# A planned order that prefers older inputs, more low parts on VectorE, and all turns of late units by DMA, in a block-sparse attention and FFN kernel

## The chip, the cores and the metric

The kernel runs on one core of a Trainium2 chip. The metric is device time of one execution in microseconds. The time of the kernel before is the median of three runs; one more execution was profiled.

## What is computed

Attention over a block mask, and an ELU feed-forward layer on its output:

```python
# q, k, v: (4, 8, 768, 64) float32 = B, H, S, D; sampled_blocks: (24, 3) int64; block = 32
scores = (1/sqrt(D)) * q @ k^T                    # per batch and head
mask   = |block_i - block_j| <= 1, or i or j the first or last block,
         or j one of the 3 blocks sampled for block row i
attn   = softmax(where(mask, scores, -1e9));  y = attn @ v
x      = y.transpose(0, 2, 1, 3).reshape(3072, 512)
h      = x @ w_in                                 # 512 x 2048, float64
g      = where(h > 0, h, exp(min(h, 0)) - 1)
out    = g @ w_out                                # 2048 x 512, float64; out (3072, 512) float32
```

## The kernel before, in words

**Split numbers.** Products are made of fp16 parts. A float is cast to fp16 (the high part) and the rest, value minus high part, is a second fp16 (the low part); a product takes three matmuls, high by high, high by low, low by high. So nearly every operand goes through two operations: a cast (`scaled`, L295 to L301, on ScalarE at L297 or on VectorE at L299) and a low part (for `p` L822, for `g` L902, for `xn` L866, for weights L462), which may run on VectorE or GpSimd. The weights are float64, decoded from their bits by ScalarE and VectorE (L427 to L463).

**Attention.** `attention` (L658) handles a unit of 128 query rows and all 8 heads. There are 24 units. Most hold two blocks of each of two batches; units 0 and 1 are of one batch; units 8 and 20 hold the first and last blocks, which attend to every key, so they have three chunks of scores (`NC = 3`, L762). Units 0 to 11 belong to the first two batches, 12 to 23 to the others. For each pair of heads (`hp`, four of them) a unit makes scores (L788, 32 narrow matmuls of 32 columns of weights, or more), their maximum (L799, VectorE), two exponentials (L817, ScalarE), the cast of `p` (L297 or L299), its low part (L822), the turn of `p` into `pT`, P·V (L837) and a sum into `x32` (L846, VectorE). At the end of a unit the rows are divided by their sums (L854 to L856), split into `xn` and turned into `xT`.

**Turns.** `turn16` (L374) turns eight 128x128 tiles of fp16. Either by the transfer engine, one DMA issued on SP (L377), or by eight TensorE transposes into a PSUM bank (L385) and an eviction by ScalarE or VectorE (L387 to L391). `via` (L951) says which: for units 0 to 3 everything on TensorE; from unit 4 on q and `xn` by DMA, and `p` of the first two head pairs (`hp < via[1]`, `PP = 2`, L825) on TensorE, of the other two by DMA.

**FFN.** `ffn` (L872) handles two units, a stage `U` of 256 rows, in eight steps: layer 1 (L885, 24 wide matmuls into `h`), ELU (L895, L897 on ScalarE, L893 on VectorE), the cast and low part of `g`, and layer 2 (L908, 6 matmuls into each of two `o` banks). At the end of a stage two evictions go into `ro` (L918) and are stored from SP (L642). There is one `ro` buffer (`rooms`, L260), so the second eviction needs the first store to have landed.

**What sets the order.** No engine's order is written out. Each operation is added with a priority (a time in us at which it is wanted, worked out from `t`, the stage's time, by constants such as `AHEAD`, `T`, `F2`, `LAG`, `K1`), with the engines it may run on and a duration on each. `Plan.order` (L70) then goes through a planned time `t` and gives each engine, when it is free, the first operation in the order of priority that is ready: its inputs ended `LATENCY` ago, and its buffers have room. An engine that isn't free in time keeps what it would finish sooner than another by a margin (L113 to L120); `MO` is the margin of low parts, and a low part goes to the engine that ends it first, with VectorE set back by it. So a change of a constant moves operations on all engines, and between them. Every engine then executes its list in order on the chip, waiting where an input isn't there.

Of the kernel before, what the change touches and what calls it, by code (L numbers as in the profile page):

```python
# [17 lines left out]

LATENCY = 0.15
LANDING = 2.5  # L20
IN_FLIGHT = 8
BACKLOG = 3.5
FETCH, FETCH_TIME = 256, 5.0
PACE, SLACK = 0.0, 0.1
SWITCH, HERD, HOLD = 0.1, 1, 0.7


# [15 lines left out]
class Plan:  # L43
# [26 lines left out]
    def order(self):  # L70
# [5 lines left out]
        made = {tag: [] for tag in self.rooms}  # L76
# [30 lines left out]
        def ready(op, eng):  # L107
# [31 lines left out]
        while left:  # L139
            moved = False  # L140
            for eng, ops in waiting.items():
# [84 lines left out]
def kernel(  # L226
# [37 lines left out]
    plan = Plan(rooms)  # L264
# [37 lines left out]

    ALONE, SPECIAL, SECOND = 1, 8, -110.0
    MO, MC, ML, MH = -0.6, 0.0, 0.5, 0.6

# [352 lines left out]
    def attention(u, t, via):  # L658
        g, i0, blocks = unit(u)
        sp = i0 == 0  # L660
        PITCH, TURN, TIMES = (PI, TU, TM) if u >= EVEN else (1.0, 2.0, 4.0)
        keys_in = [k for x in {b for b, _ in blocks} for k in kT_buf[x]]
        tq = t - 9 - AHEAD

# [22 lines left out]
        if sp:  # L687
            vts = [Buf("VT", lambda: None) for _ in range(3)]

            def take(e):  # L690
                for vt in vts:
                    vt.slot = next_slot()
                    in_room["v", vt.slot] = None
            plan.add({"SP": 0.01}, t - 8, take, new=vts, name=f"vt{u}")
            for c in range(NKC):
                vt = vts[c // 2]

                def load(e, c=c, vt=vt):
                    r0 = BLK + c * P
                    for d, xs in vd[g]:  # L700
# [6 lines left out]
                plan.add({"SP": 0.45 * len(vd[g])}, t - 8, load, r=[d for d, _ in vd[g]], w=[vt], dma=1.6, name=f"vt{u}")  # L707
            vin = vts
        else:
# [3 lines left out]
            for y in range(2):  # L713
# [7 lines left out]
                def load(e, vt=vt, parts=parts):  # L721
# [3 lines left out]
                    for d, xs, i in parts:  # L725
# [4 lines left out]
                        nc.sync.dma_start(room[BLK:P, 1], d.ap[(i - 1) * BLK : (i + 2) * BLK, :])  # L730
                plan.add({"SP": 0.6 * len(parts)}, t - 8, load, r=[d for d, _ in there], new=[vt], dma=1.8, name=f"vt{u}")
# [6 lines left out]
                plan.add({"POOL": 1.0 * len(parts)}, t - 8, gather, r=[d for d, _ in there], w=[vt], dma=1.7, land=5.0, port=False, name=f"vg{u}")  # L738

                def copy(e, kg=kg, y=y):  # L740
# [4 lines left out]
                    for x in range(2):  # L745
# [13 lines left out]
                plan.add({"POOL": 1.75 if two else 2.5}, t - 6, copy, r=keys_in, new=[kg], name=f"kg{u}")  # L759

# [162 lines left out]
    SHIFT = {"ACT": 0.6, "DVE": 0.7}  # L923
    EVEN, NEXT = 6, 14.0
    PI, TU, TM = 2.0, 3.0, 4.0
    TWO, AHEAD, T, F0, LEAD, NPE = 6, 16.0, 58.0, 60.0, 130.0, 4
    WI, WID, F2, LAG = -100.0, 3.0, 4.5, 14.0
    V1, K1 = 70.0, 16.0
    QP, PP, XP = 0, 2, 0
    zero_rows(-480)  # L930
# [10 lines left out]
    for U in range(NU // 2):  # L941
        t = F0 + T * U
        for u in (2 * U, 2 * U + 1):
            at = t - LEAD + (T / 2 if U else NEXT) * (u % 2)
            if u == NUP:
# [39 lines left out]
```

## Time and profile before

| | |
|---|---|
| median of three runs | 823.76 us (820.37 to 824.18) |
| the profiled execution: its span | 807.9 us |
| busy shares of the span: TensorE, VectorE, ScalarE, GpSimd | 88%, 63%, 53%, 49% |
| instructions | 26664 |
| moved by DMA | 120.07 MB, mean 149 GB/s |

The profile gives the profiled execution's own time as its span, from the first to the last instruction; the runs' times are some 16 us longer, as they hold what lies around the span. "Busy" is the time in which an engine executed something; the share is a mean over stages with different limits. In the page of the profile a first stretch to about 140 us, in which weights and keys are prepared, has TensorE busy for four to eight tenths; then it is busy for nine tenths and more of nearly every slice until the last one.

### The profile page before, as it was taken

What the parts mean: (1) busy time and instruction counts of PE and PEld (TensorE: products, weight loads), DVE (VectorE), ACT (ScalarE), POOL (GpSimd) and SP (SyncE); (2) the same over time, 40 slices, a digit from 0 to 9 for tenths busy, and PEclk for the clock granted to TensorE, in tenths of its full rate; (3) what the DMA queues carried; (4) which work ended last, traced back from release to release, by engine and by line L of the source; (5) the groups of instructions that cost most, each with busy time, mean ns of one, the idle gap of its engine ahead of it and who ended that gap; (6) DMA issues with size and microseconds to landing.
All of it is one profiled execution on the core that took longest, in us unless ns stands there. A gap on an engine that the chain in (4) does not pass through costs nothing.

```text
span 807.9 us, 26664 instructions
## 1 busy us (share of the span) xinstructions
PE 711.3 (88%) x11256; PEld 488.3 (60%) x11256; DVE 506.4 (63%) x854; ACT 428.9 (53%) x747; POOL 392.7 (49%) x600
## 2 busy tenths in 40 slices
PE   6445665999998999899899998999999999999993
PEld 3333553767657657567567656656667576566761
DVE  7689788998876747666478766647555566522210
ACT  4598777888545636355466525445345346322220
POOL 2587657687534347543565535445324464422120
PEclk8555578999999999999999999999999999999997
DMA  8898999988787789999459987464761698210000
GB/s 231 248 281 277 264 263 212 217 204 163 134 179 223 169 148 209 172 170 200 94 106 182 162 176 93 110 131 42 172 114 15 94 208 146 41 40 1 28 1 26
DMA packets 191064, 120.07 MB, mean 149 GB/s; under 512 B 148000, under 2 KB 168608, under 8 KB 190944
## 3 DMA queue, kind: packets, MB, share of 16 engines
q1 hardware_dynamic: 185664, 100.79, 61.0%
q0 software_dynamic: 5280, 17.58, 8.5%
q8 instruction: 88, 1.44, 0.8%
q14 instruction: 32, 0.26, 0.1%
HBM read 82.05 MB, written 13.21 MB: 118 GB/s over the span
## 4 chain that ended last, share of the span: by engine, by line
PE 66%; DMA 14%; DVE 6%; issue 4%; ACT 3%; POOL 2%; SPq 2%; POOLq 1%; DVEq 0%; ACTq 0%
PE o L908 27%; PE h L885 25%; PE s L788 5%; DMA out_dram<-ro 5%; PE w L837 3%; DMA pT<-p 2%; PE av L837 2%; DMA wo<-in_moe_w_out_dram 2%; DMA st<-in_k_dram 2%; PE av L385 2%; DMA VT<-vd 1%; PE s L385 1%; DMA st<-in_v_dram 1%; ACT e L817 1%; DVE w L451 1%
## 5 line engine op out<-in xcount | busy, mean ns | idle before, releaser
L885 PE MATMUL h<-xT,wi 128*128 128x256 f16 x2304 | 280.4, 275 | 7.8 <-DVE fe L893 4.7
L908 PE MATMUL o<-wo,g 128*128 128x512 f16 x1152 | 274.6, 381 | 0.0
L885 PEld LDWEIGHTS <-wi 128*128 128x128 f16 x2304 | 220.2, 98 | 53.9 <-issue 9.0
L902 POOL TENSOR_TENSOR g<-fe,g 128x512 f16<-128x512 f32 x79 | 96.0, 1215 | 188.8 <-DVE g L299 167.8
L908 PEld LDWEIGHTS <-g 128*128 128x128 f16 x1152 | 107.5, 98 | 109.2 <-issue 1.6
L822 POOL TENSOR_TENSOR p<-e,p 128x512 f16<-128x512 f32 x86 | 102.3, 1193 | 88.6 <-DVE p L299 44.9
L895 ACT ACTIVATE fe<-h 128x512 f32<-128x512 f32 x96 | 57.3, 597 | 148.4 <-PE h L885 145.7
L893 DVE SCALAR_TENSOR_TENSOR fe<-h,fe 128x512 f32<-128x512 f32 x96 | 66.0, 688 | 107.8 <-ACT fe L897 100.1
L817 ACT ACTIVATE e<-s,m 128x256 f32<-128x256 f32 x208 | 86.1, 471 | 68.4 <-POOL p L822 25.4
L757 POOL COPY kG<-kT 128x128 int32 x264 | 76.3, 331 | 41.6 <-PE s L788 18.6
L799 DVE TENSOR_REDUCE m<-s 128x2 f32<-128x512 f32 x104 | 69.8, 685 | 36.0 <-PE s L788 35.7
L735 POOL DMA_INDIRECT VT<-vd,idx x66 | 65.5, 992 | 27.6 <-issue 9.1
L837 PEld LDWEIGHTS <-pT 128*32 128x32 f16 x3456 | 42.8, 97 | 47.3 <-issue 34.6
L897 ACT ACTIVATE fe<-fe,gs 128x512 f32<-128x512 f32 x96 | 69.3, 722 | 2.4
L788 PE MATMUL s<-kG,qT 128*32 128x160 f16 x704 | 44.5, 249 | 10.6 <-ACT e L817 6.3
L788 PEld LDWEIGHTS <-qT 128*32 128x32 f16 x1664 | 33.2, 101 | 28.9 <-issue 21.5
L846 DVE TENSOR_REDUCE x<-w 128x130 f32<-128x260 f32 x64 | 27.2, 425 | 33.6 <-PE w L837 33.2
L788 PE MATMUL s<-kT,qS 128*32 128x96 f16 (+1 forms) x832 | 48.2, 226 | 0.0
L788 PE MATMUL s<-kT,qT 128*32 128x96 f16 (+1 forms) x832 | 48.1, 227 | 0.0
L788 PE MATMUL s<-kG,qS 128*32 128x160 f16 x704 | 44.2, 248 | 4.0 <-DVE qS L299 2.7
L299 DVE CAST p<-e 128x512 f16<-128x512 f32 x54 | 32.4, 603 | 19.2 <-ACT e L817 6.3
L385 PEld LDWEIGHTS <-p 128*128 128x128 f16 x512 | 34.5, 105 | 15.9 <-POOL p L822 7.7
(134 smaller groups left out, 859.9 us busy)
## 6 DMA issues: line engine op xcount, KB each, us to landing
VT<-vd SPq DMA_DIRECT2D x44, 195.0 KB
VT<-vd SPq DMA_DIRECT2D x22, 390.0 KB
wo<-in_moe_w_out_dram SPq DMA_DIRECT2D x12, 512.0 KB
out_dram<-ro SPq DMA_DIRECT2D x21, 256.0 KB
st<-in_q_dram SPq DMA_DIRECT2D x40, 128.0 KB
wo<-in_moe_w_in_dram SPq DMA_DIRECT2D x9, 512.0 KB
st<-in_moe_w_in_dram SPq DMA_DIRECT2D x7, 512.0 KB
VT<-vd SPq DMA_DIRECT2D x12, 260.0 KB
```

Source lines behind the costliest of these rows:

```text
L735: nc.gpsimd.indirect_dma_start(VT[0:96, 2 * vt.slot, xs[0] : xs[-1] + 1].rearrange("p b x -> p (b x)"), None, d.ap, bass.IndirectOffsetOnA ...
L757: nc.gpsimd.tensor_copy(dst[:, :, r * 16 : (r + 1) * 16], src[:, :, bass.ds(at[r], 16)])
L788: nc.tensor.matmul(dst, lhsT=qq.ap[:, h, j * BLK : (j + 1) * BLK], rhs=mv, start=first, stop=(y == 1 and qq is qS and o0 + w == 256))
L799: nc.vector.tensor_reduce(m.ap[:, 2 * c : 2 * c + 2] if sp else m.ap[:, 6:8], ss[c].ap, axis=AX.X, op=ALU.max, negate=True)
L817: nc.scalar.activation(e32.ap[:, y, :], ss[c].ap[:, y, :], AF.Exp, bias=m.ap[:, 6 + y : 7 + y])
L822: plan.add(LO, t + PITCH * hp + 1, margin=MO, fn=lambda e, e32=e32, p=p: ENG[e].tensor_tensor(p.ap[:, 1, :], flat(e32.ap), p.ap[:, 0, :], ...
L837: nc.tensor.matmul(av.ap[j * BLK : (j + 1) * BLK, y, v0:], lhsT=pts[c].ap[:, pl * 4 + y * 2 + z, j * BLK : (j + 1) * BLK], rhs=VT[:, room, ...
L885: nc.tensor.matmul(h.ap[:, a, :], lhsT=w[:, wl, cs], rhs=x.ap[:, xl, cc, :], start=(n == 0), stop=(n == 3 * NCC - 1))
L893: nc.vector.scalar_tensor_tensor(e32.ap, h.ap, -IH * GS, e32.ap, op0=ALU.mult, op1=ALU.min)
L897: plan.add({"ACT": 0.68}, p0 + 2.6, lambda e, e32=e32: nc.scalar.activation(e32.ap, e32.ap, AF.Relu, bias=gs_col, scale=-GS), r=[e32], w=[ ...
L902: plan.add(LO, p0 + 2.6, margin=MO, fn=lambda e, e32=e32, g=g: ENG[e].tensor_tensor(g.ap[:, 1], e32.ap, g.ap[:, 0], op=ALU.subtract), r=[e ...
L908: nc.tensor.matmul(o.ap, lhsT=g.ap[:, gl, f % 2, m * P : (m + 1) * P], rhs=wo[f][:, wl, :], start=(f == 0 and n == 0), stop=(f == NFC - 1 ...
```

## The change

The constants go to the top of the file, and most change a little. Four things are new:

- `eased`: in the planned time behind `EASE_FROM = 140`, an operation of TensorE whose inputs from other engines ended less than 1.04 us ago (3.03 for a DMA), or whose buffer came free so recently, gets 10 added to its rank. So one whose inputs were ready for longer goes first, if there is one.
- `TURNED = 14`: from unit 14 on no head pair's `p` is turned on TensorE. Units 4 to 13 stay as they were.
- `MARGIN`: `MO`, the margin of low parts, goes from -0.6 to -0.06. The other three stay.
- The assumed latency between engines goes from 0.15 to 0.04, the backlog of transfers from 3.5 to 1.72, and the stages are ranked by new constants (`AHEAD`, `T`, `F2`, `LAG`, `WID`, `K1`, and the time of q).

```diff
-LATENCY = 0.15
+LATENCY = 0.04
-BACKLOG = 3.5
+BACKLOG = 1.72
+MARGIN = (-0.06, 0.0, 0.5, 0.6)
+PITCH1 = (2.0, 3.16, 4.0)
+TWO, AHEAD, T, F0, LEAD, NPE = 6, 17.58, 60.83, 60.0, 130.0, 4
+WI, WID, F2, LAG = -100.0, 2.93, 4.73, 15.05
+TURNED = 14
+EASE, EASE_DMA, EASE_FROM = 1.04, 3.03, 140.0
...
+        def eased(op):
+            for d in op.deps:
+                if d.eng != "PE" and d.end + (EASE_DMA if d.dma else EASE) > t:
+                    return False
+            for b in op.new:
+                if b.tag is None:
+                    continue
+                i = len(made[b.tag]) - self.rooms[b.tag]
+                if i >= 0 and any(o.end + EASE > t for o in (*made[b.tag][i].writers, *made[b.tag][i].readers) if o.eng != "PE"):
+                    return False
+            return True
...
                         s = fetch(op)[0] + hurry(op) + (0.0 if op.narrow or not narrow or HERD < 2 else SWITCH)
+                        if t > EASE_FROM and not eased(op):
+                            s += 10.0
...
-    MO, MC, ML, MH = -0.6, 0.0, 0.5, 0.6
+    MO, MC, ML, MH = MARGIN
...
-        tq = t - 9 - AHEAD
+        tq = t - QLEAD - AHEAD
...
-    TWO, AHEAD, T, F0, LEAD, NPE = 6, 16.0, 58.0, 60.0, 130.0, 4
-    WI, WID, F2, LAG = -100.0, 3.0, 4.5, 14.0
...
-            attention(u, at, ("PE", 4, "PE") if u < NPE else (("DMA", "PE")[QP], PP, ("DMA", "PE")[XP]))
+            attention(u, at, ("PE", 4, "PE") if u < NPE else ("DMA", 2 if u < TURNED else 0, "DMA"))
```

Lines behind the constants stand 26 lower in the changed file: L385 becomes L411, L822 L848, L902 L928, L885 L911.

How this moves instructions, at three places. First the SP queue around units 16 and 17 (`pT` is the turned `p`, `VT` gathered values, `st` loaded rows of q, `out_dram` the result). Before:

```order
L377 DMA_TRANSPOSE pT_11203<-p_11089 128x8x128
L377 DMA_TRANSPOSE pT_11280<-p_11166 128x8x128
L642 DMA out_dram<-ro_11241 2x64x512
L642 DMA st_11404<-in_q_dram 64x8x64 x2
L730 DMA VT<-vd_191 96x2080 x2
L377 DMA_TRANSPOSE pT_11643<-p_11592 128x8x128
L377 DMA_TRANSPOSE qT_11698<-n_10626 128x8x128
L377 DMA_TRANSPOSE pT_11798<-p_11739 128x8x128
```

And after the change:

```order
L403 DMA_TRANSPOSE pT_11060<-p_11029 128x8x128
L403 DMA_TRANSPOSE pT_11118<-p_11058 128x8x128
L403 DMA_TRANSPOSE qT_11170<-n_10084 128x8x128
L668 DMA out_dram<-ro_11135 2x64x512
L403 DMA_TRANSPOSE xT_10719<-xn_11225 128x8x128
L403 DMA_TRANSPOSE pT_11327<-p_11235 128x8x128
L403 DMA_TRANSPOSE pT_11357<-p_11249 128x8x128
L756 DMA VT<-vd_192 96x2080 x2
L403 DMA_TRANSPOSE pT_11648<-p_11525 128x8x128
L403 DMA_TRANSPOSE pT_11692<-p_11584 128x8x128
```

Unit 17 has four turns of `p` in the queue instead of two, and the output store stands behind two turns of `p` and one of q.

Second, VectorE in unit 17, at the operations for `p` and for `g` of the stage beside it. Before:

```order
L893 SCALAR_TENSOR_TENSOR fe_11337<-h_11282,fe_11337 128x512
L299 CAST g_11352<-fe_11337 128x512
L497 SCALAR_TENSOR_TENSOR n_11317<-st_9858,n_11317 128x8x64
L846 TENSOR_REDUCE x_11149<-w_11356 128x130
L822 TENSOR_TENSOR p_11354<-e_11299,p_11354 128x512
L299 CAST p_11417<-e_11348 128x512
L893 SCALAR_TENSOR_TENSOR fe_11415<-h_11322,fe_11415 128x512
```

And after the change:

```order
L919 SCALAR_TENSOR_TENSOR fe_11392<-h_11208,fe_11392 128x512
L325 CAST g_11436<-fe_11392 128x512
L928 TENSOR_TENSOR g_11436<-fe_11392,g_11436 128x512
L825 TENSOR_REDUCE m_11487<-s_11403 128x2
L825 TENSOR_REDUCE m_11523<-s_11440 128x2
L848 TENSOR_TENSOR p_11525<-e_11331,p_11525 128x512
L325 CAST p_11584<-e_11352 128x512
L848 TENSOR_TENSOR p_11584<-e_11352,p_11584 128x512
```

Before, the low parts of `g_11352` and `p_11417` were on GpSimd; now each follows its cast on VectorE. In the whole program 143 low parts go that way: of `p` 86 are on GpSimd before and 20 now, of `g` 79 and 27, of `xn` 11 and 2, of weights 19 and 3. TensorE has 192 transposes fewer.

Third, ScalarE at the two evictions at the end of stage 7 (`ro` is the buffer of which there is one, `fe` and `g` belong to ELU steps of the next stage, `n` to a cast of q, `e` to exponentials). Before:

```order
L895 ACTIVATE fe_13370<-h_13283 128x512
L897 ACTIVATE fe_13370<-fe_13370,gs 128x512
L297 ACTIVATE g_13421<-fe_13370 128x512
L297 ACTIVATE ro_13425<-o_12634 128x512
L895 ACTIVATE fe_13441<-h_13357 128x512
L817 ACTIVATE e_13444<-s_13305,m_13355 128x256 x2
```

And after the change:

```order
L921 ACTIVATE fe_12920<-h_12828 128x512
L923 ACTIVATE fe_12920<-fe_12920,gs 128x512
L323 ACTIVATE n_12932<-st_12841 128x8x64
L323 ACTIVATE ro_13041<-o_12260 128x512
L323 ACTIVATE n_13094<-st_12909 128x8x64
L323 ACTIVATE ro_13112<-o_12290 128x512
L921 ACTIVATE fe_13147<-h_13080 128x512
L923 ACTIVATE fe_13147<-fe_13147,gs 128x512
```

Before, one of the two evictions was on ScalarE and the other on VectorE; now both are on ScalarE, one cast apart.

## Rows read from the trace of the kernel before

**Rows 1.** Busy time of each engine by window. The columns: the window, its length, busy time of PE, PEld, DVE, ACT and POOL with the number of instructions, the granted TensorE clock, the busy share of the DMA engines, GB/s.

```profile
60.00:193.00 133.00, 99.49 (x1976) 72.91 (x1976) 118.17 (x176) 107.50 (x188) 93.17 (x146) 0.80 0.96 234
...
0.00:100.00 100.00, 53.28 (x897) 39.92 (x897) 80.81 (x132) 71.22 (x117) 61.08 (x130) 0.59 0.91 260
100.00:140.00 40.00, 25.45 (x565) 19.20 (x565) 34.69 (x52) 30.72 (x54) 26.83 (x38) 0.80 1.05 241
140.00:193.00 53.00, 52.13 (x929) 36.60 (x927) 47.69 (x76) 44.71 (x82) 37.60 (x64) 0.99 0.92 202
193.00:720.00 527.00, 505.86 (x8377) 344.37 (x8375) 327.12 (x568) 263.30 (x468) 250.41 (x358) 1.00 0.73 137
720.00:808.00 88.00, 74.58 (x496) 48.23 (x493) 16.14 (x29) 18.93 (x29) 16.81 (x15) 0.95 0.05 16
```

**Rows 2.** The page: busy time and share of each engine, then the chain of waits by engine.

```profile
PE 711.3 (88%) x11256; PEld 488.3 (60%) x11256; DVE 506.4 (63%) x854; ACT 428.9 (53%) x747; POOL 392.7 (49%) x600
...
PE 66%; DMA 14%; DVE 6%; issue 4%; ACT 3%; POOL 2%; SPq 2%; POOLq 1%; DVEq 0%; ACTq 0%
```

**Rows 3.** TensorE's waits from 150 to 808 us, the first five of fourteen rows: the operation that waited, what it waited for, us in total, times, longest.

```profile
PE s L385 <- DVE n L497: 3.6, 2, 3.0
PE h L885 <- DVE g L299: 3.0, 1, 3.0
PE av L837 <- DVE pT L299: 2.7, 2, 2.1
PE w L837 <- DMA pT<-p: 2.5, 2, 1.4
PE s L788 <- DVE fe L893: 1.6, 1, 1.6
```

**Rows 4.** The chain of waits, pieces of the stretches around 245 us and around 480 us (start, length, what).

```profile
245.57 10.40 DMA out_dram<-ro
...
480.09 10.91 DMA out_dram<-ro
491.02 0.60 ACT ro L297
491.62 0.62 ACT fe L897
492.26 0.70 DVE fe L893
492.98 0.44 DVE g L299
493.74 4.09 PE h L885 x36
```

**Rows 5.** The chain of waits, single pieces between 427 and 455 us.

```profile
427.96 0.45 PE s L788 x26
...
435.73 1.29 PE o L908 x6
437.02 0.46 PE w L837 x32
437.48 1.42 PE h L885 x12
438.90 0.45 PE av L385 x8
...
441.69 0.55 PE av L385 x8
442.25 0.56 PE s L788 x32
...
454.68 1.31 PE h L885 x12
```

**Rows 6.** Groups of instructions by line and shape, whole span: count, busy us, mean ns of one, idle time before them and what ended it.

```profile
L385 PE MATMUL av<-ident,p 128*128 128x128 f16 x256 | 19.7, 220 | 0.2 <-PE w L837 0.2
L297 ACT ACTIVATE pT<-av 128x1024 f16<-128x1024 f16 x27 | 27.6, 1023 | 12.0 <-PE av L385 11.5 <-issue 0.4
L822 DVE TENSOR_TENSOR p<-e,p 128x512 f16<-128x512 f32 x26 | 23.2, 891 | 2.7 <-issue 1.5 <-ACT p L297 1.0
L299 DVE CAST p<-e 128x512 f16<-128x512 f32 x54 | 32.4, 603 | 19.2 <-ACT e L817 6.3 <-DMA pT<-p 5.0 <-PE s L385 3.1
L799 DVE TENSOR_REDUCE m<-s 128x2 f32<-128x512 f32 x104 | 69.8, 685 | 36.0 <-PE s L788 35.7
L817 ACT ACTIVATE e<-s,m 128x256 f32<-128x256 f32 x208 | 86.1, 471 | 68.4 <-POOL p L822 25.4 <-DVE m L799 24.6 <-PE o L908 7.0
```

**Rows 7.** The tiles `p`, `g` and `pT`: count, duration in ns (min, median, max), first and last start.

```profile
L822 POOL TENSOR_TENSOR p<-e,p x86: 1142/1160/1650, 43.8 to 693.3; 128x512 f16<-128x512 f32 x86
L299 DVE CAST p<-e x54: 413/427/2577, 44.5 to 688.6; 128x512 f16<-128x512 f32 x54
L377 SPq DMA_TRANSPOSE pT<-p x48: 1231/1316/5028, 157.7 to 694.4; - x48
L822 DVE TENSOR_TENSOR p<-e,p x26: 674/692/1741, 96.5 to 681.8; 128x512 f16<-128x512 f32 x26
...
L902 POOL TENSOR_TENSOR g<-fe,g x79: 1145/1156/1672, 135.6 to 788.4; 128x512 f16<-128x512 f32 x79
L902 DVE TENSOR_TENSOR g<-fe,g x17: 680/693/1531, 144.3 to 566.8; 128x512 f16<-128x512 f32 x17
```

**Rows 8.** Turns by DMA: two pieces of the chain of waits, then SP's timeline of unit 20 (start, length in the queue, count).

```profile
545.36 9.02 DMA pT<-p
...
678.40 10.13 DMA pT<-p
...
623.82 3.39 SPq L377 DMA_TRANSPOSE pT<-p  x2
627.33 1.26 SPq L377 DMA_TRANSPOSE qT<-n  x1
630.93 11.37 SPq L377 DMA_TRANSPOSE pT<-p  x4
```

**Rows 9.** The chain of waits where stage 1 begins.

```profile
183.18 1.01 PE s L788 x64
184.18 2.73 PE h L885 x24
```

More of the change, by code (lines that the diff above doesn't have):

```diff
@@ L17 @@
 WINDOW = 1
-LATENCY = 0.15
+LATENCY = 0.04
 LANDING = 2.5
 IN_FLIGHT = 8
-BACKLOG = 3.5
+BACKLOG = 1.72
+MARGIN = (-0.06, 0.0, 0.5, 0.6)
+SECOND = -110.0
+EVEN, NEXT = 6, 14.0
+PITCH0 = (1.0, 2.0, 4.0)
+PITCH1 = (2.0, 3.16, 4.0)
+TWO, AHEAD, T, F0, LEAD, NPE = 6, 17.58, 60.83, 60.0, 130.0, 4
+WI, WID, F2, LAG = -100.0, 2.93, 4.73, 15.05
+V1, K1 = 70.0, 20.28
+VLEAD, KLEAD, QLEAD = 8.0, 6.0, 8.23
+TURNED = 14
 FETCH, FETCH_TIME = 256, 5.0
@@ L301, in scaled @@
             ENG[eng].tensor_scalar(dst, src, scale, None, op0=ALU.mult)
-    ALONE, SPECIAL, SECOND = 1, 8, -110.0
-    MO, MC, ML, MH = -0.6, 0.0, 0.5, 0.6
+    ALONE, SPECIAL = 1, 8
+    MO, MC, ML, MH = MARGIN
     gs_col = const([P, 1], F32, "gs")
@@ L660, in attention @@
         sp = i0 == 0
-        PITCH, TURN, TIMES = (PI, TU, TM) if u >= EVEN else (1.0, 2.0, 4.0)
+        PITCH, TURN, TIMES = PITCH1 if u >= EVEN else PITCH0
         keys_in = [k for x in {b for b, _ in blocks} for k in kT_buf[x]]
-        tq = t - 9 - AHEAD
+        tq = t - QLEAD - AHEAD
         s, n = buf("st2", [P, H, D], F32), buf("n2", [P, H, 2, D], F16)
@@ L693, in take @@
                     in_room["v", vt.slot] = None
-            plan.add({"SP": 0.01}, t - 8, take, new=vts, name=f"vt{u}")
+            plan.add({"SP": 0.01}, t - VLEAD, take, new=vts, name=f"vt{u}")
             for c in range(NKC):
@@ L706, in load @@
                             nc.sync.dma_start(dst[64:P], d.ap[NB * BLK :, :])
-                plan.add({"SP": 0.45 * len(vd[g])}, t - 8, load, r=[d for d, _ in vd[g]], w=[vt], dma=1.6, name=f"vt{u}")
+                plan.add({"SP": 0.45 * len(vd[g])}, t - VLEAD, load, r=[d for d, _ in vd[g]], w=[vt], dma=1.6, name=f"vt{u}")
             vin = vts
@@ L730, in load @@
                         nc.sync.dma_start(room[BLK:P, 1], d.ap[(i - 1) * BLK : (i + 2) * BLK, :])
-                plan.add({"SP": 0.6 * len(parts)}, t - 8, load, r=[d for d, _ in there], new=[vt], dma=1.8, name=f"vt{u}")
+                plan.add({"SP": 0.6 * len(parts)}, t - VLEAD, load, r=[d for d, _ in there], new=[vt], dma=1.8, name=f"vt{u}")
                 def gather(e, vt=vt, parts=parts):
@@ L737, in gather @@
                             bass.IndirectOffsetOnAxis(ap=idx[0:96, i : i + 1], axis=0))
-                plan.add({"POOL": 1.0 * len(parts)}, t - 8, gather, r=[d for d, _ in there], w=[vt], dma=1.7, land=5.0, port=False, name=f"vg{u}")
+                plan.add({"POOL": 1.0 * len(parts)}, t - VLEAD, gather, r=[d for d, _ in there], w=[vt], dma=1.7, land=5.0, port=False, name=f"vg{u}")
                 def copy(e, kg=kg, y=y):
@@ L758, in copy @@
                                 dst[:, :, r * 16 : (r + 1) * 16], src[:, :, bass.ds(at[r], 16)])
-                plan.add({"POOL": 1.75 if two else 2.5}, t - 6, copy, r=keys_in, new=[kg], name=f"kg{u}")
+                plan.add({"POOL": 1.75 if two else 2.5}, t - KLEAD, copy, r=keys_in, new=[kg], name=f"kg{u}")
         x32 = buf("x32", [P, H, D + 1], F32)
@@ L923 @@
     SHIFT = {"ACT": 0.6, "DVE": 0.7}
-    EVEN, NEXT = 6, 14.0
-    PI, TU, TM = 2.0, 3.0, 4.0
-    TWO, AHEAD, T, F0, LEAD, NPE = 6, 16.0, 58.0, 60.0, 130.0, 4
-    WI, WID, F2, LAG = -100.0, 3.0, 4.5, 14.0
-    V1, K1 = 70.0, 16.0
-    QP, PP, XP = 0, 2, 0
     zero_rows(-480)
```

## The prediction

> **What bounds the kernel now.** I read the windows by stage first, because the share of busy time mixes stages with different limits [rows 1]. Up to 140 us TensorE stands idle for 46.7 + 14.6 = 61.3 us, and the granted clock is 0.59 and 0.80 there: weights, keys and the first units are being prepared. From 140 to 720 us it is idle for only 0.9 + 21.1 = 22.0 us at a granted clock of 0.99 to 1.00; the tail adds 13.4 us. So from 140 us on the kernel is bound by the number of rows TensorE executes, and ahead of that by whatever readies stage 1. From 60 to 193 us VectorE is busy for 118.2 of 133.0 us, 89%, more than ScalarE (81%) or GpSimd (70%). Over the whole span VectorE has 506.4 us in 854 instructions, 0.593 us each, and GpSimd 392.7 us [rows 2].
>
> The waits of TensorE come next [rows 3]. The five largest of the fourteen rows make 13.4 of the 22.0 us: a score or turn behind a low part of q or k (3.6), a layer-1 product behind `g` (3.0), turns and P·V behind `pT` (2.7 and 2.5), a score behind `fe` (1.6). The chain of waits shows where the 3.0 us come from [rows 4]: a store of `ro` takes 10.91 us; the second `ro` eviction of its stage needs that one buffer and stands in ScalarE's queue until 491.02, with two ELU steps of a later `h` queued behind it; they, VectorE's `fe` and `g`, and at last the layer-1 products at 493.74 follow in turn. Such stores recur: another took 10.40 us at 245.57.
>
> The time is added up on the profiled span, 807.9 us. The median of the runs, 823.8 us, lies 15.9 us above it, and these 15.9 us are carried over.
>
> **The change, part by part.**
>
> *Turns.* Head pairs 0 and 1 of units 14 to 23 leave TensorE: nine units by two, and special unit 20 by two by three chunks, 24 turns of 8 transposes. A turn is one piece of 0.45 us on the chain, 0.55 right behind a wide matmul [rows 5]; by busy time it is 19.7 / 256 x 8 = 0.62 us [rows 6]. TensorE is the bound there, so the pieces come off the end: 24 x 0.45 = **-10.8 us**, at most 24 x 0.62 = -14.8. The 24 PSUM evictions that go with them (1.02 us each, mostly ScalarE's [rows 6]) lay beside that work; priced at nothing.
>
> *What the 24 turns cost as DMAs.* Each holds the SP queue for a median of 1.32 us [rows 7], 31.7 us in all; SP's own share of the chain is 2% [rows 2]. The two slowest on the chain took 9.02 and 10.13 us to land [rows 8]. From a score to its P·V the steps are a maximum of 0.69, two exponentials of 0.47, a cast of 0.43 to 0.60, a low part of 0.69 to 1.16, the issue of 1.32 and up to 10.13: 14.2 to 14.8 us at worst [rows 6 to 8]. What TensorE has to do in between, added up along the changed order with 1.31 us for a layer-1 group, 1.3 for layer 2, 0.56 for scores and 0.46 for P·V [rows 5], is 14.4 us in the tightest of these units, 15.7 in the next, and 18 and over in nearly all. So it is hidden: nothing. If that cover is gone in one unit, the unit pays half a microsecond; a second limit, the two `p` buffers, is a rival below. On SP the output stores now stand behind two turns of `p` and one of q; if a turn waits for its low part, the store behind it starts later and the `ro` chain above grows. This I keep in the bound of the waits.
>
> The row for a turn shows 0.45 us on TensorE and 9 to 10 us by DMA in slow cases. The Trainium skill (VectorE: DVE Perf Modes, Rules for kernel authors) says to turn 128x128 tiles on TensorE where PSUM can take them, and its Three transpose paths give 1.309 us to the DMA for one tile: an estimate of 10.5 us for a turn of eight. Two of the rows agree with it, but six turns issued within 18.5 us [rows 8] do not. By that rule the turns would become the bound, which is the second rival.
>
> *Switches between narrow and wide work.* A layer-1 group behind narrow work takes 1.42 us and otherwise 1.31; scores take 0.56 behind wide work and 0.45 behind narrow [rows 5]. Of these pairs, 0.11 + 0.10 = 0.21 us each, the new order has eight fewer behind stage 1: **-1.7 us**.
>
> *Waits of TensorE.* From 140 us on, an operation whose inputs are younger than 1.04 us (3.03 for a DMA) in the planner's time is put behind any that waited longer. That aims at the short waits of rows 3. It cannot touch the `ro` chain: there is still one `ro` buffer, and at stage 7 the two evictions now both stand on ScalarE with one `n` between them, so everything behind the second waits for a store as before. I put about half of the 22.0 us down to that chain (four stores of 8 to 11 us, 3 us of TensorE each) and take half of the rest: **-6 us**. The bounds are -15 (all but two stalls gone) and +5 (a stall of 3.0 more and one of 2 where two stores meet).
>
> *VectorE.* The margin of low parts falls from -0.6 to -0.06, and 143 of them leave GpSimd for VectorE: 66 of `p`, 52 of `g`, 9 of `xn`, 16 of weights. GpSimd loses 143 x 1.16 = 166 us and VectorE gains 143 x 0.69 = 99 us [rows 7]. Behind 193 us VectorE has 200 us free in 527 [rows 1]; nothing. Ahead of it it hasn't. In the new order 37 low parts instead of 15 stand ahead of the norm of unit 3 on VectorE, that is 22 more by 0.69 to 0.89 us (its median and mean for `p` [rows 6, 7]): 15.2 to 19.6 us, against 133.0 - 118.2 = 14.8 us free. The excess is 0.4 to 4.8 us; I take **+4 us**, near the mean, since casts there are stretched already. The bounds: +15, if none of the free time can be used (22 x 0.69), and -15, since the last weight's VectorE step has 26 VectorE rows fewer ahead of it (26 x 0.593) and the chain at 184 us [rows 9] would start that much sooner. TensorE itself has 2.4 us less work ahead of stage 1, which I leave in this span.
>
> The cast of `p` takes 0.413 us at the least, 0.427 at the median and 2.577 at the most, a mean of 0.603 [rows 6, 7]: it is held up now and then. The Trainium skill (SBUF — State Buffer, SBUF: two separate sides) has a reason: VectorE and GpSimd share a pair of ports, and whoever has it keeps it for a whole instruction. By that rule moving low parts to VectorE gives back some of this, for the casts of `p` alone 54 x (0.603 - 0.427) = 9.5 us, and the startup term would be 0 or below; the first rival below is its time.
>
> *Sum:* -10.8 - 1.7 - 6 + 4 = -14.5 us. Span 793.4, time **809 us**.
>
> **The rivals.**
>
> 1. *VectorE is freed rather than loaded.* Stretched casts shrink by 9.5 us as GpSimd falls quiet, and stage 1 starts 6 us sooner instead of 4 later: 809 - 10 = 799 us. For it: the spread of the casts. Against: 89% busy already. Chance 0.20.
>
> 2. *The change doesn't do what it says for TensorE.* The waits are those of stores, the rule of age finds nothing to better, and startup costs its 4.8 with some more: -10.8 - 1.7 + 5 + 6 = -1.5, 822 us. For it: rows 4 and the unchanged buffer. Chance 0.15.
>
> 3. *VectorE becomes the bound (slower).* It decides when the added low parts exceed VectorE's free time: 15.2 against 14.8 us ahead of 193 us, so it is at that point now. With casts of `p` at their mean and none of the free time usable, startup costs 13 us; behind it each `fe` and `g` waits one low part (0.69) longer for a share of 96 groups, 15 of them exposed, +10: -10.8 - 1.7 + 10 + 13 = +10.5, 834 us. Against: 38% of VectorE is free behind 193 us. Chance 0.08.
>
> 4. *Turning by DMA becomes the bound (slower).* Two `p` buffers are free again only when their turn has landed. Units 14 to 23 now have 48 turns, 24 pairs. TensorE has 275.7 us of work from the first scores of unit 14 to the last P·V of unit 23, added up as above; so it decides from a cycle of 275.7 / 24 = 11.5 us. A cast, a low part, an issue and 10.13 us of landing come to 12.6 to 13.2. At 13 us it is 312, 36 us more: 845 us. Against: six turns in 18.5 us are a cycle of 6.2. Chance 0.05.
>
> **How the numbers follow.** The forecast has what is left, 0.52, with a range of its own of 801 to 817. A measurement of this kernel tells about 0.5% from no change, 4.1 us: under 819.6 is faster, over 827.9 slower. The forecast and the first rival are faster, with a few hundredths of the second, 0.74; the second gives most of 0.13 for the same; rivals 3 and 4 make 0.13 slower. The range, 794 to 825, takes in the first two rivals; it leaves out the two slower ones, 0.13, and a few hundredths for the low ends of waits and startup together.
>
> **What would show it.** Right: TensorE's busy time down by about 12 us; stage 1's first layer-1 product at 180 to 190 us; TensorE idle 12 to 18 us from 140 to 720 us with stores still in front of `ro`; few waits on `pT` by DMA. Wrong in the direction of 1: casts of `p` near 0.43 on the mean and stage 1 before 180 us. Of 3: waits of TensorE on `fe` and `g` by VectorE, which is over 95% busy ahead of stage 1. Of 4: TensorE waiting for `pT` behind 450 us by tens of microseconds. The forecast is wrong as a whole if stage 1 starts more than 10 us away from 184 us.

## The result, and the profile after

The changed kernel takes 827.92 us (825.09 to 834.84, 13 runs) where the kernel before takes 824.24 (819.25 to 827.85, 13 runs): a ratio of 1.0062 [1.0040, 1.0084]. In a second comparison on another chip it is 1.0031 [1.0004, 1.0058]. The forecast was 809; the change costs 2.5 to 5 us instead.

One number has to be put right first. The kernel before takes 824 us on some chips and 812 to 814 on others, so times are compared only through ratios on one chip. The first profile's span, 807.9, lies among the spans of before on the quicker chips (803.9 to 814.9) and not among those on the others (819.0 to 826.5); which chip it was taken on isn't on record. In the runs whose span is known the time lies 1.7 to 2.5 us above it (1.7 to 1.8 for these two kernels), so the 15.9 us that stand beside the times of before as lying around the span, and that the prediction carried over, were not there. The table therefore holds two profiles of each kernel: those compared are the second of before with the first of the changed kernel, and the other way round. "Half clock" is the time at a granted clock of 0.5.

| us | before, 1st | before, 2nd | changed, 1st | changed, 2nd |
|---|---|---|---|---|
| span | 807.9 | 823.0 | 826.2 | 811.7 |
| first layer-1 product of stage 1 | 184.1 | 186.9 | 191.1 | 188.1 |
| TensorE idle ahead of it | 62.1 | 61.7 | 71.6 | 70.3 |
| TensorE idle from it to the last layer-1 product | 21.2 | 26.8 | 28.9 | 27.5 |
| half clock in that stretch | 3.4 | 13.7 | 27.3 | 13.7 |
| from the last layer-1 product to the end | 22.6 | 22.6 | 22.6 | 22.6 |

823.0 to 826.2 adds up: stage 1 starts 4.2 later; TensorE's idle time behind it is 2.1 longer; its busy time there is 3.2 shorter (586.7 to 583.5): +3.1, where 3.2 was measured. Those 3.2 fit three terms: half clock +13.6, which at half speed loses 6.8; the 2.4 us of work that the prediction saw leaving the startup, and that now come behind it; and its -12.5 for turns and switches. Together they make -3.3. The idle time is read from these windows, of before (second profile: 13.9 + 12.2 + 0.7 = 26.8) and then of the changed kernel (first: 16.0 + 9.9 + 3.0 = 28.9), columns as in [rows 1]:

```profile
193.00:491.00 298.00, 284.08 (x4675) 190.69 (x4673) 195.62 (x339) 154.80 (x275) 146.55 (x223) 0.99 0.82 161
491.00:720.00 229.00, 216.83 (x3624) 147.71 (x3623) 127.36 (x227) 105.62 (x189) 102.66 (x138) 0.99 0.56 105
720.00:800.00 80.00, 79.30 (x556) 54.18 (x555) 19.09 (x34) 20.97 (x32) 18.44 (x16) 1.00 0.06 18
```

```profile
193.00:498.00 305.00, 289.02 (x4835) 195.24 (x4833) 215.04 (x384) 161.74 (x289) 92.13 (x188) 0.98 0.82 158
498.00:720.00 222.00, 212.11 (x3449) 140.75 (x3447) 146.53 (x267) 95.35 (x183) 44.41 (x88) 0.98 0.84 143
720.00:804.00 84.00, 80.98 (x737) 55.79 (x735) 35.28 (x59) 25.87 (x43) 3.48 (x3) 0.98 0.21 32
```

The same windows as in [rows 1], of the changed kernel:

```profile
60.00:193.00 133.00, 94.89 (x1685) 67.26 (x1686) 104.69 (x175) 99.48 (x172) 63.15 (x104) 0.74 0.82 210
0.00:100.00 100.00, 43.78 (x701) 31.08 (x705) 70.48 (x128) 68.26 (x111) 48.79 (x111) 0.60 0.91 257
100.00:140.00 40.00, 27.55 (x491) 21.36 (x480) 31.77 (x53) 31.16 (x53) 16.27 (x25) 0.68 0.96 240
140.00:193.00 53.00, 50.05 (x834) 32.63 (x832) 47.00 (x78) 40.18 (x72) 24.35 (x43) 0.97 0.65 149
193.00:720.00 527.00, 501.14 (x8282) 335.99 (x8280) 361.56 (x650) 257.08 (x472) 136.54 (x276) 0.98 0.83 152
```

VectorE is busy for 104.7 us of 60 to 193, less than before (118.2): the startup was not lost to a full VectorE. From 193 us on the granted clock is 0.98 where [rows 1] has 1.00.

TensorE's waits in the changed kernel from 150 to 808 us, the five largest of eleven rows, to hold beside [rows 3]:

```profile
PE s L814 <- issue: 8.1, 13, 1.9
PE h L911 <- DVE fe L919: 5.7, 3, 3.0
PE w L863 <- DVE x L872: 3.9, 2, 3.0
PE s L411 <- DVE n L523: 3.8, 3, 2.4
PE av L863 <- DMA pT<-p: 2.9, 1, 2.9
```

Four long stalls make up most of the waits on `fe` (2.5 and 3.0 us), on `x` (3.0) and on `pT` (2.9). The chain of waits shows what is behind them, as in [rows 4]:

```profile
598.92 7.84 DMA out_dram<-ro
606.87 0.60 ACT ro L323
607.46 0.50 ACT fe L921
607.98 0.73 ACT fe L923
608.74 0.70 DVE fe L919
609.48 5.76 PE h L911 x36
...
619.07 13.14 DMA pT<-p
...
663.69 8.37 DMA out_dram<-ro
...
721.12 8.26 DMA out_dram<-ro
```

Three stores of `ro`, and a turn that took 13.14 us. The turn was issued at 619.07 behind a second store (607.49, landed at 615.95), a turn of `xn` that held SP's queue for 6.59 us, and seven loads. The products at 609.48 take 5.76 us for three groups, where three take 3 x 1.31 = 3.93 [rows 5]: behind the stall TensorE ran at 1.2 GHz for a while. The windows there (columns as above; 0.57 is a mean of the two levels):

```profile
606.00:610.00 4.00, 1.54 (x42) 1.19 (x40) 1.87 (x4) 3.02 (x5) 0.00 (x0) 1.00 0.19 34
610.00:614.00 4.00, 4.00 (x24) 2.94 (x23) 3.27 (x8) 2.85 (x7) 2.10 (x2) 0.57 2.55 286
614.00:618.00 4.00, 4.00 (x55) 2.72 (x53) 1.46 (x3) 1.87 (x4) 0.00 (x0) 1.00 0.13 47
```

TensorE was idle for 2.46 us up to 609.48, fell to half clock behind it, and was back at 614. Behind stage 1's start the changed kernel has eight such stretches in its first profile and three in its second; before has one and three. Each of the four long stalls in its first profile has one, but not every stall does: in [rows 4] a stall of 3.0 us is followed by three groups in 4.09 us, at full clock. The mean granted clock of all runs points the same way as the profiles: its median is 0.911 and 0.915 for the changed kernel in the two comparisons, 0.925 and 0.929 for before on the chips of its second profile and of the second comparison.

### The profile page after: what moved, and what is told of

The parts are those of the page before. It is cut to its first block, busy times and chain, and to the rows that moved or that the text cites. A ratio compares the mean times of both kernels' runs of the same rounds, so it can differ in the third digit from the quotient of the medians.

```text
span 826.2 us, 26178 instructions
## 1 busy us (share of the span) xinstructions
PE 712.4 (86%) x11064; PEld 480.7 (58%) x11064; DVE 547.9 (66%) x968; ACT 424.9 (51%) x752; POOL 229.4 (28%) x457
## 4 chain that ended last, share of the span: by engine, by line
PE 67%; DMA 12%; DVE 9%; issue 3%; ACT 3%; POOL 2%; SPq 2%; POOLq 0%; another core or an unknown queue 0%; DVEq 0%; ACTq 0%
PE h L911 27%; PE o L934 26%; PE s L814 5%; DMA out_dram<-ro 4%; PE w L863 3%; PE av L863 2%; DMA pT<-p 2%; PE s L411 1%; DMA VT<-vd 1%; DMA wo<-in_moe_w_out_dram 1%; DMA wo<-in_k_dram 1%; DVE w L477 1%; DVE fe L919 1%; PE av L411 1%; DMA st<-in_v_dram 1%
## 5 line engine op out<-in xcount | busy, mean ns | idle before, releaser
L911 PE MATMUL h<-xT,wi 128*128 128x256 f16 x2304 | 289.7, 280 | 11.9 <-DVE fe L919 9.9
L911 PEld LDWEIGHTS <-wi 128*128 128x128 f16 x2304 | 225.5, 100 | 64.8 <-issue 14.9
L783 POOL COPY kG<-kT 128x128 int32 x264 | 80.8, 350 | 193.0 <-PE s L814 172.3
L843 ACT ACTIVATE e<-s,m 128x256 f32<-128x256 f32 x208 | 85.8, 469 | 56.9 <-DVE m L825 26.9
L848 DVE TENSOR_TENSOR p<-e,p 128x512 f16<-128x512 f32 x92 | 67.5, 735 | 6.5 <-ACT p L323 4.7
L928 POOL TENSOR_TENSOR g<-fe,g 128x512 f16<-128x512 f32 x27 | 34.0, 1259 | 126.1 <-DVE g L325 73.3
L814 PE MATMUL s<-kG,qT 128*32 128x160 f16 x704 | 44.5, 247 | 12.6 <-ACT e L843 10.7
L928 DVE TENSOR_TENSOR g<-fe,g 128x512 f16<-128x512 f32 x69 | 49.0, 710 | 3.9 <-ACT g L323 1.5
L323 ACT ACTIVATE ro<-o 128x512 f32<-128x512 f32 x19 | 11.3, 597 | 64.7 <-PE o L934 52.3
```

The costliest lines, as they stand in the source:

```text
L783: nc.gpsimd.tensor_copy(dst[:, :, r * 16 : (r + 1) * 16], src[:, :, bass.ds(at[r], 16)])
L814: nc.tensor.matmul(dst, lhsT=qq.ap[:, h, j * BLK : (j + 1) * BLK], rhs=mv, start=first, stop=(y == 1 and qq is qS and o0 + w == 256))
L843: nc.scalar.activation(e32.ap[:, y, :], ss[c].ap[:, y, :], AF.Exp, bias=m.ap[:, 6 + y : 7 + y])
L848: plan.add(LO, t + PITCH * hp + 1, margin=MO, fn=lambda e, e32=e32, p=p: ENG[e].tensor_tensor(p.ap[:, 1, :], flat(e32.ap), p.ap[:, 0, :], ...
L911: nc.tensor.matmul(h.ap[:, a, :], lhsT=w[:, wl, cs], rhs=x.ap[:, xl, cc, :], start=(n == 0), stop=(n == 3 * NCC - 1))
L928: plan.add(LO, p0 + 2.6, margin=MO, fn=lambda e, e32=e32, g=g: ENG[e].tensor_tensor(g.ap[:, 1], e32.ap, g.ap[:, 0], op=ALU.subtract), r=[e ...
```

## The experiments

Ratios are to the kernel before on the same chip, five rounds each, with 95% intervals.

**Before again.** No edit.

> The kernel before, unchanged, for a second profile. The first one has a span of 807.9 us, 16 below the median of the runs, while the changed kernel's profile (826.2) lies 1.7 below its own. Theory A, the first profile was an exceptionally fast execution: the new span is 819 to 824, stage 1 starts within 3 us of 184, and TensorE shows six or more stretches at half clock behind 150 us instead of one. Theory B, the 16 us lie outside the span: the span is 806 to 811 again with one such stretch.

Span 823.0, time 824.74; three stretches at half clock, 13.7 us in all, stage 1 at 186.9. That is the span that theory A had, with half as many stretches at half clock: the first profile isn't typical of a chip on which before takes 824 us. Whether it was an unusual execution or one on a quicker chip the runs don't say.

**One part alone, or undone: the turns.**

In before, the turns alone (first); in the changed kernel, all but the turns (second).

```diff
-attention(u, at, ("PE", 4, "PE") if u < NPE else (("DMA", "PE")[QP], PP, ("DMA", "PE")[XP]))
+attention(u, at, ("PE", 4, "PE") if u < NPE else ("DMA", 2 if u < 14 else 0, "DMA"))
```

```diff
-TURNED = 14
+TURNED = 24
```

> The kernel before with one part of the change: p of units 14 to 23 turned by DMA alone. Its order is that of before up to unit 14. If the turns come off the end as forecast (24 x 0.45 us on a TensorE that has no other bound there), the time is 10 to 12 us lower, ratio 0.986. If what they give back is lost to waits on pT and to stretches at half clock behind them, ratio 0.995 to 1.005. If turning by DMA is the bound, ratio over 1.02.

> The changed kernel without that part: the first two head pairs of units 14 to 23 are turned on TensorE as before, all else as changed; the order is the changed one's up to unit 14. If the turns by DMA are worth their 11 us there too, it takes 835 to 841 us (ratio to before 1.014 to 1.02). If the DMA turns are what costs the changed kernel its time, it is as fast as before or faster (ratio up to 1.0).

Alone 0.9928 [0.9899, 0.9958], 5.9 us. Undone, 1.0140 [1.0101, 1.0180] where the changed kernel has 1.0062: 6.4 us. So the turns by DMA help in both orders, by a little over half of the 10.8 us. The profile of the first says where the rest can go: span 819.6 against 823.0, idle behind stage 1 the same (26.9 and 26.8), but half clock 23.9 against 13.7, which loses 5.1, and stage 1 2.2 later in the same order. TensorE's busy time behind stage 1, less what half clock loses, falls by 10.9 us there (586.7 - 6.8 to 580.9 - 12.0), so as work the 10.8 were right. That execution is one of the slower of its seven, at a clock of 0.917 where their median is 0.922: the median run lost less to half clock than this one.

**The rule of age undone, and added to before.**

```diff
-EASE, EASE_DMA, EASE_FROM = 1.04, 3.03, 140.0
+EASE, EASE_DMA, EASE_FROM = 1.04, 3.03, 1e9
```

That is the first; the second is before with `eased`, its +10 and the turns; the third is the first with LATENCY 0.15 and BACKLOG 3.5.

> The changed kernel without the rule of age. Theory E, the rule breaks up TensorE's order: the waits that nothing in the profile explains (9.5 us behind 150 us, 3 before) and the stretches at half clock behind them (nine, one before) go, 8 to 15 us less than the changed kernel, ratio to before 0.985 to 0.995. Theory S, the loss is made ahead of stage 1 (191 us against 184) and the rule costs nothing: ratio 1.0 to 1.01, like the changed kernel's 1.006.

> The kernel before with the rule of age and with p of units 14 to 23 turned by DMA, and nothing else: margin, latency, backlog and stage constants are those of before, so the order ahead of 140 us of planned time is too. If the startup is what the changed kernel loses, this one keeps before's (stage 1 at 184 to 189 us) and the rule takes some of the waits behind it: 806 to 816 us, ratio 0.978 to 0.99, below the 0.993 of the turns alone. If the rule only mends what the lower latency of the changed kernel broke, it adds nothing here: ratio 0.99 to 1.0.

> The changed kernel without the rule of age and with the old latency (0.15) and backlog (3.5). Without the rule and with the new ones the ratio was 1.0298; with rule and old ones 0.9933. If the rule only mends what the short latency breaks: 0.993 to 1.003, TensorE idle for 20 to 28 us between stage 1's start and the last layer-1 product. If the rule is worth its 2% in any order of the new constants: 1.01 to 1.02, idle 35 us or more.

Without it 1.0298 [1.0265, 1.0331]: both theories missed, in this order the rule saves 2%. TensorE is idle for 44.7 us behind stage 1, and the largest row of its waits from 190 to 815 us is for turns:

```profile
PE w L863 <- DMA pT<-p: 19.2, 4, 8.0
```

But added to before, with the turns, it brings nothing: 0.9926 [0.9900, 0.9952]. And with the old latency and backlog the changed kernel is better without it, 0.9860 [0.9832, 0.9889], than with it, 0.9933 (on another chip). There the same row of its waits reads:

```profile
PE w L863 <- DMA pT<-p: 4.0, 2, 2.4
```

So with stores as they are the rule only mends what the short latency and backlog do: with them P·V waits for turns by DMA for 19.2 us, without them for 4.0. Which of the two does it was not run.

**The other parts undone in the changed kernel.** Old margin (first), old latency and backlog (second), the old margin for weights and units 0 to 3 only (third), the old stage constants (fourth), old margin, latency and backlog (fifth), the old backlog alone (sixth); and the changed kernel again (seventh). The lines of the first two edits; the constants go back to the values in the section on the change, with K1 at 16.0 and the time of q at 9.0:

```diff
-MARGIN = (-0.06, 0.0, 0.5, 0.6)
+MARGIN = (-0.6, 0.0, 0.5, 0.6)
-LATENCY = 0.04
+LATENCY = 0.15
-BACKLOG = 1.72
+BACKLOG = 3.5
```

> The changed kernel with the old margin of low parts (-0.6), so 194 instead of 52 of them are on GpSimd. Theory M, the startup is lost by the margin: TensorE idles 71.6 us ahead of stage 1 in the changed kernel and 61.7 in the second profile of before; with the old margin it is 60 to 64, stage 1 starts 6 to 10 us sooner and the time is 817 to 822 (ratio to before 0.99 to 0.997). Theory L, it is lost by the new latency, backlog or stage constants: idle time ahead of stage 1 stays at 69 to 76 and the ratio at 1.0 or above. Theory P (shared port): casts of p on VectorE are longer again by 0.1 us or more on the mean than in the changed kernel.

> The changed kernel with the planner's old latency (0.15) and old backlog of transfers (3.5). Theory L, these two cost the startup: idle time of TensorE ahead of stage 1 falls from 71.6 to about 62 us, and the time by 8 to 10 us, ratio to before 0.99 to 0.997. Theory M or the stage constants: it stays at 69 to 76, ratio 1.0 to 1.01.

> The changed kernel with the old margin for the low parts of weights and of units 0 to 3 only; all later ones keep the new margin. If theory M is right and its place is the startup, idle time ahead of stage 1 is 60 to 64 us as with the old margin everywhere, and the time 815 to 820 us. If the margin is not the cause, 69 to 76 us and a ratio of 1.0 or above.

> The changed kernel with the old stage constants (PITCH1, AHEAD, T, WID, F2, LAG, K1, the time of q); latency, backlog, margin, rule of age and turns as changed. Undoing the margin and undoing latency with backlog each left TensorE idle for 71 to 72 us ahead of stage 1, so by elimination theory C: the constants cost the startup. Then idle time ahead of stage 1 is 60 to 65 us and the ratio 0.985 to 0.995. If each part costs some of it only in company with the others: 68 to 74 us, ratio 0.99 to 1.005.

> The changed kernel with old latency, backlog and margin: it differs from before by the stage constants, the rule of age and the turns, and from the kernel with rule and turns alone (ratio 0.9926) by the stage constants. Theory C: the constants cost 8 us or more, ratio over 1.0, idle time ahead of stage 1 70 us or more. Theory of company: ratio 0.985 to 0.995, idle time 60 to 66 us.

> The changed kernel with the old backlog (3.5) alone; the latency stays at 0.04. Undoing both gave 0.9933. If the backlog was the cause of that, because transfers queue up sooner and the values for the first units come in time: ratio 0.99 to 0.997. If the latency was, because operations planned 0.04 us behind each other arrive late on the chip: the ratio stays at 1.0 to 1.01.

> The changed kernel, unchanged, beside the kernel before on one chip. Before took 824 us in one comparison and 814 in another, so its times differ by chip. If the changed kernel's loss is its own: ratio 1.004 to 1.008 again, stage 1 at 187 to 192 us, five or more stretches at half clock behind it. If the loss belonged to the chip of the first comparison: ratio 0.99 to 1.0.

| undone | ratio | idle ahead of stage 1 |
|---|---|---|
| nothing | 1.0031 [1.0004, 1.0058] | 70.3 |
| margin | 0.9961 [0.9930, 0.9993] | 72.2 |
| margin at the start | 0.9953 [0.9926, 0.9980] | 72.6 |
| latency, backlog | 0.9933 [0.9912, 0.9955] | 71.3 |
| backlog | 0.9962 [0.9929, 0.9994] | 77.8 |
| constants | 1.0019 [0.9994, 1.0045] | 75.2 |
| margin, latency, backlog | 0.9984 [0.9957, 1.0011] | 61.9 |

The rows of the margin, of the margin at the start, and of latency with backlog are from one chip, on which the changed kernel itself was not run, the others from another. In idle time theories M, L and C each fall: the 62 us of before come back only when margin, latency and backlog are all old (also 63.2 and 61.2 in before with the turns, and with turns and rule). With the new constants the new margin alone, or new latency and backlog alone, costs the 10 us. In time M and L came out as expected (0.9961 and 0.9933, each said 0.99 to 0.997), though not by the startup. And where the startup is back at 61.9 the theory of company missed: the ratio is 0.9984, with 29.6 us of idle time and 30.7 us at half clock behind stage 1. So a shorter startup alone didn't make the kernel faster. How this looks in the first profile of the changed kernel: rows of the timelines of GpSimd, ScalarE and VectorE (start, length, instruction, in the bracket the idle time before it and what ended it), then the largest row of TensorE's waits from 55 to 115 us.

```profile
60.87 0.95 POOL L761 DMA_INDIRECT VT<-vd,idx  x1 [0.16 <-issue]
62.12 0.92 POOL L761 DMA_INDIRECT VT<-vd,idx  x1 [0.30 <-issue]
63.05 2.28 POOL L848 TENSOR_TENSOR p<-e,p 128x512 f16<-128x512 f32 x2
```

```profile
64.93 1.02 ACT L323 ACTIVATE pT<-o 128x1024 f16<-128x1024 f16 x1 [7.44 <-PE o L411]
```

```profile
68.69 1.25 DVE L488 TENSOR_TENSOR wo<-wo 128x512 f16<-128x512 f32 x1 [8.37 <-ACT wo L323]
```

```profile
PE o L411 <- POOL p L848: 15.5, 4, 11.3
```

A low part of `p` stands on GpSimd behind gathers and copies of keys; TensorE's turn waits for it (11.3 us at once), ScalarE's eviction for the turn, and a weight's low part on VectorE for a cast queued behind that eviction. Each queue waits in its order; none is full. In the second profile of before the same kind of wait is 3.5 us in all. Why the planner makes this order and not another is not settled.

**Stores.** A two-batch store as two DMAs of 64 rows in place of one of 2x64x512. `move` has the branch that loads use; the store's own branch goes. The order of every engine stays, and lines behind the store stand two higher. Done to four orders of the above, the changed kernel's first, and to before alone:

```diff
-        elif i and store:
-            parts = [(far[b : b + 2, i * BLK : (i + 2) * BLK], tile_)]
         elif i:
             parts = [(far[b + x, i * BLK : (i + 2) * BLK], tile_[64 * x : 64 * x + 64]) for x in range(2)]
```

> The changed kernel, order of every engine unchanged, but each output store of a unit of two batches is issued as two DMAs of 64 rows instead of one of 2x64x512 (these landed 7.8 to 12.1 us after issue, the last one on the tail in 7.9). Theory W, the waits I forecast as falling are store waits that stay: the stalls of TensorE of 2.48, 2.99 and 3.10 us behind such stores go (-8 us), the tail ends 5 to 6 us sooner, and the stretches at half clock right behind these stalls go too (1.7 us each, -5): ratio to before 0.978 to 0.985. If the half clock costs nothing of itself: 0.985 to 0.988. If the second DMA on SP's queue costs what the first saves: over 0.995.

> The kernel before with the turns by DMA, the rule of age and the stores as two DMAs each; margin, latency, backlog and stage constants are those of before. Without the new stores its ratio was 0.9926. Theory W: the tail gives 5 to 6 us and the stalls behind stores with their half clock 5 to 8: ratio 0.976 to 0.982. If its stores weren't waited for inside the run, the tail alone: 0.985 to 0.987.

> The changed kernel with the old latency and backlog (ratio 0.9933) and the stores as two DMAs each: the same 10 to 14 us of tail, stalls and half clock: 0.975 to 0.982; the tail alone 0.986.

> The kernel before with its stores as two DMAs each and nothing else. With the same stores the changed kernel has a ratio of 0.9595. If the change is worth what I forecast (about -1.8%) once stores are quick, this one is at 0.975 to 0.981, and the changed order gains more from quick stores (35 us) than the old one (15 to 20). If quick stores are worth the same 35 us in the old order, it is at 0.955 to 0.962 and the change gives nothing.

> The changed kernel without the rule of age, with the old latency and backlog (ratio 0.986), and the stores as two DMAs each. If stores are worth 25 us and more in each order, it is the fastest, 0.95 to 0.957. If without the rule its waits are of another kind (turns by DMA, scores), the stores give the tail's 8 us and little else: 0.965 to 0.976, behind the changed kernel with quick stores.

| with the stores | ratio | without them |
|---|---|---|
| changed kernel | 0.9595 [0.9570, 0.9620] | 1.0062 and 1.0031 |
| before with turns and rule | 0.9669 [0.9641, 0.9696] | 0.9926 |
| changed, old latency and backlog | 0.9869 [0.9829, 0.9909] | 0.9933 |
| before | 0.9610 [0.9578, 0.9642] | 1 |
| changed, old latency and backlog, no rule | 0.9540 [0.9511, 0.9568] | 0.9860 |

The changed kernel goes from 826.2 to 792.6 us of span with the same order on every engine and the same start of stage 1 (191.1 and 191.4). Idle time behind it falls from 28.9 to 12.2 us, half clock from 27.3 to 10.2 (8.5 lost), the end from 22.6 to 14.2: 16.7 + 8.5 + 8.4 = 33.6, all of the difference. TensorE's busy time behind stage 1 falls by 8.6 us with the same instructions, as half of the 17.1 us less at half clock should give. My expectation had half of the whole, since it counted three stalls; the wait on `pT` went too, and most of those on `x` (3.9 to 0.5) and `n` (3.8 to 1.1). Two windows of it, columns as before:

```profile
492.00:720.00 228.00, 227.72 (x3726) 153.52 (x3723) 158.91 (x286) 104.84 (x201) 47.91 (x90) 1.00 0.75 149
720.00:778.00 58.00, 58.00 (x458) 38.98 (x456) 23.36 (x39) 15.73 (x24) 1.16 (x1) 1.00 0.07 15
```

TensorE is idle for 0.3 us there, at full clock. In before's order with the new stores it is idle for 2.8 us from stage 1 to the last layer-1 product, with no stretch at half clock, and these are all its waits of that stretch over 0.15 us:

```profile
PE s L786 <- ACT e L815: 1.9, 2, 0.9
PE av L385 <- DVE x L844: 0.5, 1, 0.5
PE o L906 <- issue: 0.2, 1, 0.2
```

The third of the table missed its expectation: its order has 17.9 us of idle time up to 496 us and seven stretches at half clock left, 5.5 us of the waits for turns of `xn` by DMA; why it gains only 0.6% stays open. The fastest kernel is the last, 775.39 us against 812.07 on its chip, 4.6% ahead of before: turns by DMA, new stage constants and margin, old latency and backlog, no rule, new stores. On the same chip before with the new stores takes 781.11, so of the 4.6% the new order has 0.7. Before's and the last's row ran on another chip than the first three, so 0.9595 and 0.9610 say that the change is worth nothing clear with quick stores, not that it is worth exactly that; nor do the turns and the rule show a gain there (0.9669 against 0.9610).

## Why the prediction was wrong

Against the second profile of before the span was to fall by 14.5 us and rose by 3.2. Of these 17.7 us the waits make 8.1 (+2.1 instead of -6), half clock 6.8, and 2.4 are work that left the startup and came back behind it, which I named and priced at nothing.

The point on the port below rests on three rows. The first two are casts and low parts of `p` in the changed kernel, to hold beside [rows 6]; the third is the low part of `p` with the old margin (-0.6):

```profile
L325 DVE CAST p<-e 128x512 f16<-128x512 f32 x49 | 22.8, 465 | 16.2 <-DMA pT<-p 12.4 <-PE av L411 1.9 <-ACT e L843 1.8
L848 DVE TENSOR_TENSOR p<-e,p 128x512 f16<-128x512 f32 x92 | 67.5, 735 | 6.5 <-ACT p L323 4.7
```

```profile
L848 DVE TENSOR_TENSOR p<-e,p 128x512 f16<-128x512 f32 x33 | 32.7, 992 | 3.7 <-ACT p L323 3.1
```

- **Waits of TensorE, -6 us: the step that failed.** I took half of the 22.0 us for store-bound and gave the rule of age half of the rest; the idle time rose by 2.1 us instead. The store experiment on before leaves 2.8 of 21.2 us (its first profile), so nearly all of it hung on stores, also what the waits put down to `n`, `x` or `pT`. There was next to nothing for the rule to take. With the same slow stores the new order waits 28.9 us, of which 16.7 are the stores'. Rival 2 had the mechanism, at 0.15, with its 822 us a little low: that the waits are those of stores and the rule finds nothing.
- **Half clock: no term at all.** The 0.99 and 1.00 of [rows 1] behind 140 us, with one stretch of 3.4 us, gave no sign of it. It adds 6.8 us to the comparison above and is 8.5 of the 33.6 us that the stores gave back. A stall on TensorE is paid by its length and, often, by what follows at 1.2 GHz.
- **VectorE, +4 us: the size right by luck, the mechanism wrong.** Stage 1 starts 4.2 and 4.0 us later, and 2.4 us of work moved behind it. But VectorE had more free time, 28.3 us from 60 to 193 instead of 14.8: the queues block each other, with margin, latency and backlog each able to cause it.
- **The port.** The casts of `p` fell from 0.603 to 0.465 us on the mean, low parts of `p` on VectorE from 0.891 to 0.735, and VectorE's busy time rose by 41.5 us (506.4 to 547.9), not 99. Line by line, the instructions that VectorE took over, less those that it gave up, come to 113 us at before's means, and shorter instructions took 68 off. That is what the rule of the Trainium skill (SBUF — State Buffer, SBUF: two separate sides) says, and I put too little on it. With the low parts back on GpSimd the low parts of `p` on VectorE took 0.992 us and the casts of `g` 0.536 instead of 0.436; but the casts of `p` stayed at 0.465, where theory P had them longer, and the time fell rather than rose (0.9961), so VectorE's time is not what bounds the kernel.
- **Turns, -10.8 us.** Right as work of TensorE (10.9), but 5.9 us alone and 6.4 undone: part of the rest turned into half clock. Of the cover, one turn broke my worst case: 13.14 us instead of 10.13, and TensorE waited 2.9 us for it. The Trainium skill (VectorE: DVE Perf Modes, Rules for kernel authors) prefers TensorE for such tiles; here, where TensorE is the bound, the trace says otherwise by these 6 us. (What the prediction calls the second rival there is the fourth of its list.)
- **Slower, at 0.13.** Neither rival that I gave for it happened: VectorE was not the bound, and turns by DMA were one only in the kernel without the rule (19.2 us). Startup, idle time and half clock each came out positive, and together they ate the turns.

## What to carry to other kernels

Ahead of a new order, follow each repeated wait to the transfer at its head and ask why that transfer is slow; an order planned with a landing of 2.5 us (LANDING) can't mend one of 8. Give a stall on the busy engine two prices, its length and the slow stretch behind it. A change in how a list is ranked moves every queue: undoing the margin, the constants, the backlog, or latency with backlog gave 0.1% to 1% back, undoing the turns or the rule cost 0.8% and 2.3%, and the same rule costs 0.7% with the old latency and backlog. So a single part's worth in one order says little about its worth in another.

## What the hardware showed

The last store's issue on SP in the changed kernel, and with the new stores:

```profile
813.57 0.52 SPq L668 DMA_DIRECT2D out_dram<-fe  x1
```

```profile
788.44 1.10 SPq L666 DMA_DIRECT2D out_dram<-fe  x2
```

- A store of 2x64x512 took 7.8 to 8.4 us in the chains of the changed kernel; the same bytes as two DMAs of 64 rows ended TensorE's waits for them. On the tail the last two stores are issued 1.3 us apart. In the changed kernel they land 7.9 and 11.7 us after issue, and the span ends 12.6 us behind the last issue; with the new stores each of the four DMAs lands within 2.4 us, and the span ends 4.2 us behind the issue at 788.44. It is the shape and not the number of DMAs: in the changed kernel the stores of units 0 and 1, 256 KB of one batch in one DMA of 128 rows, land 2.6 and 3.2 us after issue. The Trainium skill (DMA: Bandwidth & Descriptors, Rules for kernel authors) has the reason: an outermost dimension smaller than 16 confines a DMA to at most as many engines. The traces agree: in the record of its semaphore a store of 2x64x512 ends in two late steps, 7.6 us or more after issue, and a DMA of 64 or 128 rows in sixteen.
- TensorE also stops in the middle of a group of scores with no input missing ("issue"): 4.1 to 13.5 us behind stage 1 in the kernels profiled on chips where before takes 824 us, 0.2 to 6.9 on those where it takes 812 to 814. What it waits for isn't in the profile; with the new stores such pauses, most of them in scores, are most of what the changed kernel still waits for there (9.1 of 12.2 us).
